# Three last-step additions on GpSimd, two last-step stores on ScalarE's queue, and one weight-scale transpose a run later

## The chip, the cores and the metric

The kernel runs on one core of a Trainium2 chip. A core has TensorE (matrix products into PSUM), VectorE and ScalarE (element-wise work, both read PSUM and SBUF), GpSimd (element-wise work on SBUF, and a DMA queue of its own) and SyncE (SP), which here only issues DMAs. Each engine works through its own instructions in program order and waits for others through semaphores. The metric is the device time of one execution in microseconds; the number for a kernel is the median of its runs. The time before is 871.42 us, median of 3 runs (871.37 to 873.0).

## The reference

`x` has 2048 rows of 640 values. After a layer norm without weights, two branches use the same normalized rows:

```python
xn = layernorm(x)
# A: attention, 32 heads of 192, keys and values are the last 512 of a cache of 2048
q = (xn @ wq) in heads;  k, v = last 512 rows of k_cache, v_cache
s = (softmax(q @ k.T * 192 ** -0.5) @ v, heads joined) @ wo
# B: gated unit, 640 -> 1536 -> 640
h = sigmoid(xn @ w_gate) * (xn @ w_up)
g = silu(h @ w_down)
out = x + s * g
```

There is no causal mask: every query sees all 512 keys. Everything is bfloat16 outside.

## The kernel before, in words

The schedule is written out by hand; each engine's order is the program's order. The work has three stages.

**Gated unit, first half** (to about 112 us). Row blocks of 512 are normalized, transposed and multiplied with `w_gate` and `w_up`; `h` is stored to DRAM.

**Attention** (to about 638 us). There are 16 runs, numbered r = 0 to 15, two (pi = 0 and 1) for each of eight groups g of four heads. A run has 16 score steps, k = 0 to 15 (`stage_s`, line 652), and eight products with V (`stage_pv`, line 669). Beside step k, `phase_s` (line 828) issues the query products of the next run and all side work. Queries are computed with seven products of sub-blocks where eight would be usual, in float16. Therefore the query weights are scaled by a power of two, one scale for two groups. Such a scale is made in two parts. `set_scale` (line 207) reduces partial sums on VectorE, broadcasts the value into `mx_b`, and has SP issue a 128 x 128 DMA transpose into `mx_row` (line 213). `set_scale2` (line 215) reduces that row on VectorE and makes the scale and its inverse. The dictionaries `sets` and `sets2` (lines 750 and 751) say at which (run, step) each part of the second to fourth scale stands. The scale of groups 4 and 5, the third, is first used in run 5, when ScalarE scales the weights of group 4 (line 240) among the products with V.

SP's queue carries the transposes of the attention output (line 690) and their stores (line 697), the loads of K (`load_k`, line 157) and V, the other transposes and weight loads; GpSimd's queue carries the loads of the query weights. In a run with pi = 0, step 2 issues the load of K for the next group, and step 12 scales it on VectorE (`scale_k`, line 167).

**Dense stage** (the rest). `steps` (line 770) lists 24 steps: 16 of kind O, the attention output times `wo`, and eight of kind D, `h` times `w_down`. Each takes two row tiles and does its product with seven products of sub-blocks (`product`, line 1003) in four PSUM results; two or three are kept on ScalarE first (`keep`, line 1013) and added by VectorE later. `result` (line 1033) finishes a block of one row tile (i = 0 or 1) and one column half (LEFT or RIGHT). In the second half of the O steps (m of 8 and more) it does, on VectorE: add the kept part (line 1060, where there is one), multiply by a scale and the gate (`gated`, line 991), add `acc` (line 1062, float32 inputs, bfloat16 output). The scratch `tmps` has four buffers in turn. Other O steps store a whole row tile from GpSimd's queue (line 1066); the last step stores each block as it is ready, from SP's queue (line 1064). The order in the last step is (0, LEFT), (1, RIGHT), (0, RIGHT), and (1, LEFT), which has nothing kept to add and is cut into two half-blocks of 160 columns (line 1156): five stores.

Of the kernel before, what the change touches and what calls it, by code (L numbers as in the profile page):

```python
# [9 lines left out]
ALU = mybir.AluOpType  # L10
# [7 lines left out]
def kernel(  # L18
# [13 lines left out]
    nc = tc.nc  # L32
    P = 128
# [3 lines left out]
    of = out.flatten_outer_dims()  # L37
# [54 lines left out]
    DN = D // 2  # L92
# [180 lines left out]
    with ExitStack() as bctx:  # L273
# [198 lines left out]
        for s in range(NST):  # L472
# [4 lines left out]
            for f in range(NF):  # L477
# [16 lines left out]
                if s + 1 < NST:  # L494
                    t = (s + 1) * TQ
# [251 lines left out]
    scans_pv.update({(4 + n, 7): 15 + n for n in range(NCD)})  # L747
    scans_load = {(0, 6): (11, 5), (1, 4): (12, 4), (2, 4): (13, 5), (3, 4): (14, 4)}
    scans_load.update({(4 + n, 4): (15 + n, 5 - n % 2) for n in range(NCD)})
    sets = {(1, 1): 1, (4, 1): 2, (9, 1): 3}  # L750
    sets2 = {(1, 12): 1, (5, 0): 2, (9, 12): 3}
    scale_s = {0: 2, 3: 3, 15: 4}
    q_after = {1: (0,), 2: (1,), 3: (2,), 4: (3,), 5: (4,), 6: (5, 6), 8: (7,), 10: (8,), 12: (9,), 14: (10,)}

# [24 lines left out]
    def tiles_of(j):  # L779
        kind, m = steps[j]  # L780
        if kind == "D":
            return (m, TQ + m) if m < TQ else (TQ + m, 2 * TQ + m)
        pi, q = divmod(m % 8, TQ)
        return [(2 * pi + i) * TQ + q for i in range(2)]
# [175 lines left out]
    acc = {t: acc_pool.tile([P, D], F32, name=f"acc{t}") for t in order}  # L960
# [29 lines left out]
    def gated(dst, src, gate):  # L990
        nc.vector.scalar_tensor_tensor(dst, src, descale, gate, op0=ALU.mult, op1=ALU.mult)  # L991
# [21 lines left out]
    def keep(b, dst):  # L1013
        nc.scalar.activation(dst, ps_all[:, b, 0:DN], AF.Copy)
# [9 lines left out]
    NP = len(steps)  # L1024
    tmp_at = [0, 0, 0]

    def turn_of(k, rows_):
        tmp_at[k] += 1
        return rows_[(tmp_at[k] - 1) % len(rows_)]
# [3 lines left out]
    def result(j, i, d, b, more, n0=0, n1=DN):  # L1033
        kind, m = steps[j]
        t = tiles_of(j)[i]
        ps, tt = ps_all[:, b, n0:n1], nc.vector.tensor_tensor
        if kind == "D":
            if t not in gate_of:
                gate_of[t] = turn_of(1, gate_rows)
            if more is not None:  # L1040
                v = turn_of(2, down_tmps)
                tt(v, ps, more[:], ALU.add)
                ps = v
            nc.scalar.activation(gate_of[t][:, d], ps, AF.Silu, scale=g_scale)
            if (i, d) in ((0, RIGHT), (1, LEFT)):
                nc.gpsimd.dma_start(gB_d[t * P:(t + 1) * P, :], gate_of[t])
            return
        d = slice(d.start + n0, d.start + n1)
        if m < 8:
            if more is None:  # L1050
                keep(b, acc[t][:, d])
            else:
                tt(acc[t][:, d], ps, more[:], ALU.add)
            return
        gate, o_sb = gx_rows[1, t]
        tmp = turn_of(0, tmps)[:, 0:n1 - n0]
        if more is None:
            gated(tmp, ps, gate[:, d])
        else:
            tt(tmp, ps, more[:], ALU.add)  # L1060
            gated(tmp, tmp, gate[:, d])
        tt(o_sb[:, d], tmp, acc[t][:, d], ALU.add)  # L1062
        if j == NP - 1:
            nc.sync.dma_start(of[t * P:(t + 1) * P, d], o_sb[:, d])
        elif (i, d) in ((0, RIGHT), (1, LEFT)):
            nc.gpsimd.dma_start(of[t * P:(t + 1) * P, :], o_sb)

# [30 lines left out]
    for j in range(NP):  # L1098
# [38 lines left out]
        side(j, 3)  # L1137
        product(j, Z, "A12", 3, True)
        result(j, 0, LEFT, Z, p1s)
        scales(4)  # L1140
        side(j, 4)
        product(j, X, "S3", 4, False)
        result(j, 1, RIGHT, X, p5s)
        scales(5)
        if more:
# [6 lines left out]
        side(j, 6)  # L1152
        product(j, Y, "S4", 5, False)
        result(j, 0, RIGHT, Y, u2s)
        side(j, 7)
        cuts = (0, DN) if more else (0, DN // 2, DN)
# [42 lines left out]
```

## Time and profile before

| quantity | value |
|---|---|
| median of 3 runs | 871.42 us (871.37 to 873.0) |
| the profiled execution's own time | 872.36 us |
| its span, first to last instruction | 870.2 us |
| granted TensorE clock, mean | 0.999 |
| TensorE busy | 863.0 us |
| VectorE busy | 674.5 us |
| ScalarE busy | 628.5 us |
| GpSimd busy | 234.3 us |
| bytes moved by DMA | 175.97 MB |

In the profile PE is TensorE, PEld its weight loads, DVE VectorE, ACT ScalarE, POOL GpSimd, SP SyncE; a q behind a name is that engine's instruction queue, SPq for example the DMAs that SP issues. L1007 is line 1007 of the kernel. An instruction's line gives its start, its duration, engine, line, operation, output<-inputs, sizes and count; in brackets stands the idle time before it and what ended it. The chain is the work that ended last, followed back step by step to what released it. Times in the stage view are microseconds from the span's start.

### The profile page before, as it was taken

How to read it: one execution, taken by the hardware profiler on the slowest of the kernel's cores; microseconds unless marked ns; L12 is line 12 of the kernel's file. 1: busy time of each engine (PE TensorE's matmuls, PEld its weight loads, DVE VectorE, ACT ScalarE, POOL GpSimd, SP SyncE). 2: the span in 40 equal slices, each digit the busy share in tenths (PEclk: the TensorE clock that was granted, in tenths of full speed). 3: DMA queues.
4: the chain of work that ended last, by engine and by line, in shares of the span. 5: the costliest groups of instructions: out<-in, count | busy, mean ns of one | idle time of the engine just before them, and what ended most of it. 6: DMA issues, size and time to landing. Idle time of an engine off the chain costs nothing.

```text
span 870.2 us, 19053 instructions
## 1 busy us (share of the span) xinstructions
PE 863.0 (99%) x7557; PEld 570.7 (66%) x7557; DVE 674.5 (78%) x1148; ACT 628.5 (72%) x783; POOL 234.3 (27%) x320
## 2 busy tenths in 40 slices
PE   9999999999999999999999999999999999999998
PEld 5444447576678676676676676676777777777775
DVE  6586767777877867867877867888788778889997
ACT  4766568899799799799789688647556566766552
POOL 0085076062362352352352452300000011000000
PEclk9999999999999999999999999999999999999999
DMA  9894993998998987998988967997795977676641
GB/s 280 188 248 113 240 244 82 236 138 236 219 158 233 256 170 194 223 172 225 206 144 214 199 106 193 237 206 248 163 277 179 300 240 224 212 269 222 226 134 35
DMA packets 258872, 175.97 MB, mean 202 GB/s; under 512 B 162976, under 2 KB 241440, under 8 KB 258784
## 3 DMA queue, kind: packets, MB, share of 16 engines
q1 hardware_dynamic: 253248, 157.26, 73.2%
q0 software_dynamic: 5536, 17.50, 10.0%
q8 instruction: 59, 0.97, 0.5%
q14 instruction: 29, 0.24, 0.1%
HBM read 101.71 MB, written 36.70 MB: 159 GB/s over the span
## 4 chain that ended last, share of the span: by engine, by line
PE 97%; DVE 1%; DMA 1%; SPq 0%; issue 0%; ACT 0%; DVEq 0%
PE ps_all L1007 26%; PE ps_all L569 21%; PE ps_all L677 20%; PE ps_all L663 19%; PE ps_all L484 11%; PE ps_all L387 1%; DMA kraw<-in_A_k_cache_dram 0%; DVE stats L349 0%; DVE arm L991 0%; DMA x_sb<-in_A_x_dram 0%; DVE arm L1062 0%; DVE arm L1060 0%; DVE qp L590 0%; DVE xn L364 0%; SPq L213 0%
## 5 line engine op out<-in xcount | busy, mean ns | idle before, releaser
L667 ACT ACTIVATE E<-ps_all 128x1024 bf16<-128x1024 f32 x256 | 251.4, 1023 | 92.4 <-PE ps_all L663 90.4
L663 PE MATMUL ps_all<-qT,kT 64*128 64x512 bf16 x1536 | 198.1, 376 | 0.0
L677 PEld LDWEIGHTS <-E 128*128 128x128 bf16 x2048 | 169.7, 98 | 9.2 <-issue 9.2
L677 PE MATMUL ps_all<-v_sb,E 128*128 128x193 bf16 x2048 | 174.3, 247 | 0.9 <-DVE qT L607 0.8
L607 DVE TENSOR_TENSOR qT<-ps_all,qp 128x512 bf16<-128x512 f32 x174 | 115.7, 688 | 48.2 <-PE ps_all L569 38.8
L1007 PEld LDWEIGHTS <-mid 128*128 128x128 f16 x1236 | 120.3, 98 | 46.0
L663 PEld LDWEIGHTS <-kT 64*128 64x128 bf16 x1536 | 86.5, 94 | 77.5 <-issue 3.5
L590 DVE COPY qp<-ps_all 128x512 f32<-128x512 f32 x150 | 100.5, 687 | 42.2 <-PE ps_all L569 42.2
L684 DVE TENSOR_TENSOR o_st<-ps_all,rden 128x768 bf16<-128x768 f32 x128 | 122.6, 958 | 4.4
L569 PE MATMUL ps_all<-mid 64*128 64x512 f16 (+1 forms) x840 | 106.3, 376 | 0.0
L569 PE MATMUL ps_all<-mid,arm 64*128 64x512 f16 (+1 forms) x840 | 105.5, 376 | 0.0
L569 PEld LDWEIGHTS <-mid 64*128 64x128 f16 x840 | 50.4, 94 | 42.0 <-issue 1.4
L569 PEld LDWEIGHTS <-arm 64*128 64x128 f16 x840 | 47.1, 94 | 44.6 <-issue 0.2
L1007 PE MATMUL ps_all<-arm,mid 128*128 128x320 f16 x480 | 70.4, 299 | 0.0
L808 ACT ACTIVATE mid<-mid,w_sc 128x1536 f16<-128x1536 bf16 (+1 forms) x43 | 61.4, 1451 | 0.0
L240 ACT ACTIVATE mid<-mid,w_sc 128x1536 f16<-128x1536 bf16 x37 | 58.1, 1571 | 1.1 <-DVE w_sc L218 0.7
L1007 PE MATMUL ps_all<-op,mid 128*128 128x320 f16 (+1 forms) x408 | 58.1, 295 | 0.0
L490 DVE TENSOR_TENSOR hT_sb<-ps_all,sig_sb 128x512 bf16<-128x512 f32 x48 | 32.8, 686 | 28.4 <-PE ps_all L484 20.8
L489 ACT ACTIVATE sig_sb<-ps_all 128x512 bf16<-128x512 f32 x48 | 28.4, 596 | 35.3 <-PE ps_all L484 33.8
L258 POOL TENSOR_TENSOR mid<-mid 128x384 f16<-128x384 f16 x20 | 18.1, 906 | 120.1 <-ACT mid L240 119.1
L1007 PE MATMUL ps_all<-mid 128*128 128x320 f16 x348 | 49.9, 299 | 0.0
L258 POOL TENSOR_TENSOR arm<-mid 128x384 f16<-128x384 f16 x20 | 18.1, 907 | 114.5 <-ACT mid L240 113.5
(183 smaller groups left out, 1093.1 us busy)
## 6 DMA issues: line engine op xcount, KB each, us to landing
oT_d<-oT SPq DMA_DIRECT2D x64, 384.0 KB, 4.9
mid<-oT_d SPq DMA_DIRECT2D x46, 384.0 KB, 4.0
mid<-in_A_wq_dram POOLq DMA_DIRECT2D x64, 192.0 KB, 6.7
arm<-in_A_wo_dram SPq DMA_DIRECT2D x16, 480.0 KB, 6.2
h_d<-hT_sb SPq DMA_DIRECT2D x16, 384.0 KB, 4.4
kraw<-in_A_k_cache_dram SPq DMA_DIRECT2D x32, 192.0 KB, 3.2
v_sb<-in_A_v_cache_dram SPq DMA_DIRECT2D x32, 192.0 KB, 5.5
arm<-in_A_wq_dram SPq DMA_DIRECT2D x15, 384.0 KB, 5.3
```

The source lines that it names most:

```text
L240: nc.scalar.activation(raw.bitcast(F16), raw, AF.Copy, scale=w_ups[g // 2])
L258: tt(TB, part_w(g, c, a, 1, 1), part_w(g, c, a, 0, 1), ALU.subtract)
L484: nc.tensor.matmul(gu[:, i, :], lhsT=w[:, c, f * P:(f + 1) * P], rhs=xnT[s][:, c, :], start=(c == 0), stop=(c == NCD - 1),)
L569: nc.tensor.matmul(ps_all[:, b, :], lhsT=w(r, c), rhs=x[r, c, :], start=(first and k == 0), stop=(k == len(cs) - 1), skip_group_check=True,)
L590: nc.vector.tensor_copy(dst, part(b))
L607: nc.vector.tensor_tensor(q_out(i, u, pp), part(b), t, ALU.add)
L663: nc.tensor.matmul(ps[:, b, :], lhsT=kT[h, c * PC + j, :], rhs=qT_t[r][i, j][h, pp, :], start=(j == 0), stop=(j == PC - 1),)
L667: nc.scalar.activation(E_t[r, i, pp][:, c, :, :], ps, AF.Exp, scale=scale_qk)
L677: nc.tensor.matmul(o_ps[:, q // 2, q % 2, 0:DH + 1], lhsT=E[:, c, h, q * P:(q + 1) * P], rhs=vt[:, c, 0:DH + 1], start=(c == 0), stop=(c = ...
L684: nc.vector.tensor_tensor(o_st[:, :, h * DH:(h + 1) * DH].rearrange("p (b i) d -> p b i d", b=2), o_ps[:, :, :, 0:DH], rden[:].to_broadcas ...
L808: eng.activation(t, t.bitcast(BF16), AF.Copy, scale=up)
L1007: nc.tensor.matmul(ps_all[:, b, d0:d1], lhsT=a[:, c, :], rhs=w[:, c, d0:d1], start=(start and c == 0), stop=(c == nk - 1), skip_group_chec ...
```

## The change

Three edits. (1) The two parts of the third scale move from run 4, step 1 and run 5, step 0 to run 5, steps 1 and 12, the same steps that the second and fourth scale have in runs 1 and 9. (2) In the last dense step the addition of `acc` goes from VectorE to GpSimd for the three blocks that have a kept part; the two half-blocks stay on VectorE. (3) Two of the last step's five stores go from SP's queue to ScalarE's: that of (0, RIGHT) and that of the first half-block.

```diff
-    sets = {(1, 1): 1, (4, 1): 2, (9, 1): 3}
-    sets2 = {(1, 12): 1, (5, 0): 2, (9, 12): 3}
+    sets = {(1, 1): 1, (5, 1): 2, (9, 1): 3}
+    sets2 = {(1, 12): 1, (5, 12): 2, (9, 12): 3}
...
-        tt(o_sb[:, d], tmp, acc[t][:, d], ALU.add)
+        if j == NP - 1 and more is not None:
+            nc.gpsimd.tensor_tensor(o_sb[:, d], tmp, acc[t][:, d], ALU.add)
+        else:
+            tt(o_sb[:, d], tmp, acc[t][:, d], ALU.add)
         if j == NP - 1:
-            nc.sync.dma_start(of[t * P:(t + 1) * P, d], o_sb[:, d])
+            eng = nc.scalar if i == 0 and d.start > 0 or n0 == 0 and n1 < DN else nc.sync
+            eng.dma_start(of[t * P:(t + 1) * P, d], o_sb[:, d])
```

## The prediction

> **What bounds the kernel now.** I read the head of the page first, then the chain, then the length of each attention run, then the two places that the diff touches.
>
> ```profile
> span 870.2 us, 19053 instructions
> PE 863.0 (99%) x7557; PEld 570.7 (66%) x7557; DVE 674.5 (78%) x1148; ACT 628.5 (72%) x783; POOL 234.3 (27%) x320
> ...
> PE 97%; DVE 1%; DMA 1%; SPq 0%; issue 0%; ACT 0%; DVEq 0%
> ```
>
> TensorE is busy for 863.0 of 870.2 us, and the change removes no matmul. So it can only move the 7.2 us in which TensorE stands. Attention run r goes from one first score product (L663) to the next; the stage view, TensorE alone, shows length, TensorE busy time (count), clock, DMA share and GB/s of runs 1, 4, 5 and 9:
>
> ```profile
> 156.50:189.17 32.67, 32.67 (x331) 1.00 0.98 208
> 254.60:288.38 33.78, 32.93 (x331) 1.00 0.93 194
> 288.38:321.10 32.72, 32.72 (x332) 1.00 0.95 209
> 419.43:452.14 32.71, 32.71 (x331) 1.00 0.96 186
> ```
>
> Run 4 is 1.06 us longer than run 5. It is the run with the third scale's transpose; runs 1 and 9 hold the second's and fourth's and lose nothing. The chain inside run 4, SP's queue, VectorE's wait, and the transfer rate from 268 to 278 us in quarter microseconds:
>
> ```profile
> 272.30 0.97 SPq L213
> ...
> 273.33 0.56 SPq L161
> ...
> 273.94 3.05 DMA kraw<-in_A_k_cache_dram
> ```
> ```profile
> 271.92 1.35 SPq L213 DMA_TRANSPOSE mx_row<-mx_b  x1
> ```
> ```profile
> 276.52 0.93 DVE L170 TENSOR_SCALAR k_sb<-kraw,w_sc 128x768 bf16<-128x768 bf16 x2 [1.19 <-DMA kraw<-in_A_k_cache_dram]
> ```
> ```profile
> GB/s 294 327 342 352 373 244 303 301 304 307 310 303 295 273 284 290 336 369 358 376 361 359 310 294 187 71 131 172 212 39 184 326 393 387 369 356 393 234 37 0
> ```
>
> The transpose holds SP for 1.35 us just ahead of the K load. VectorE then stands 1.19 us for that K, with query copies behind it that free PSUM, and TensorE loses 1.06 us. From 274.0 to 275.75 us the rate falls to a mean of 142 GB/s.
>
> The other place is the end, first VectorE, then SP:
>
> ```profile
> 865.02 0.55 DVE L991 SCALAR_TENSOR_TENSOR arm<-arm,w_sc 128x320 f32<-128x320 f32 x1
> 865.60 0.49 DVE L1062 TENSOR_TENSOR arm<-arm,acc 128x320 bf16<-128x320 f32 x1
> 866.08 0.38 DVE L991 SCALAR_TENSOR_TENSOR arm<-ps_all,w_sc,arm 128x160 f32<-128x160 f32 x1
> 866.50 0.33 DVE L1062 TENSOR_TENSOR arm<-arm,acc 128x160 bf16<-128x160 f32 x1
> 866.74 0.38 DVE L991 SCALAR_TENSOR_TENSOR arm<-ps_all,w_sc,arm 128x160 f32<-128x160 f32 x1
> 867.15 0.33 DVE L1062 TENSOR_TENSOR arm<-arm,acc 128x160 bf16<-128x160 f32 x1
> ```
> ```profile
> 866.85 0.99 SPq L1064 DMA_DIRECT2D out_dram<-arm  x2
> ```
>
> Up to 864.49 VectorE follows TensorE, one block per 1.63 us. The last two half-blocks leave TensorE at about 865.2 and 866.04 and find VectorE busy. The last store is issued at 867.51, lands 1.5 us later, and the closing barriers end at 870.2.
>
> **The transpose, run 4 to run 5.** What leaves run 4: four small VectorE operations after step 1, SP's 1.35 us, and the dip in the rate. Against the 345 GB/s on either side the dip costs 1.75 x (1 - 142/345) = 1.03 us of transfer. K's two halves landed at 276.5 and 277.0 and were wanted at 275.33 and about 275.8; 1.03 us earlier they come at 275.5 and 276.0. About 0.2 us of the wait is left (run 8, with a wait of 0.30 us, is 0.2 us long), worth some 0.1 us. Gain 0.95 us. Upper end: 1.06, the whole excess. Lower end: 0.1, if K must land behind the O stores anyway, the last of which landed at 275.9; in runs 2, 6 and 8 K's first half came 0.4 to 0.6 us behind that store. I take a value near the upper end because those runs show no such dip.
>
> What arrives in run 5: the same four operations, the transpose on SP at about 297.5, and at step 12 the three that read it. Behind it on SP stand one scan load, three output-weight loads, one down-weight load and the two K transposes. SP is idle from 300.79 to 306.04 there, 5.25 us for 1.35. VectorE reaches step 12 some 20.7 us into the run, at 309; the row lands at most 4.5 us after issue, at 302. I cost it at nothing, as runs 1 and 9 measure (32.67 and 32.71). If the cover fails, the price is run 4's 1.06.
>
> **Three additions on GpSimd.** They remove three 0.49 us operations from VectorE. The first two free only time that TensorE's pace leaves idle. The third, at 865.60, is in the final queue: the rest moves up 0.51 us. But GpSimd's add runs beside it, and these two block each other:
>
> ```profile
> 47.16 0.90 POOL L259 TENSOR_TENSOR mid<-mid 128x384 f16<-128x384 f16 x1
> ...
> 47.21 2.20 DVE L455 TENSOR_TENSOR mid<-mid,x_odd 64x2560 f16<-64x2560 bf16 x1
> ```
> ```profile
> 107.20 1.47 DVE L455 TENSOR_TENSOR mid<-mid,x_odd 64x2560 f16<-64x2560 bf16 x1
> ```
>
> The same operation takes 1.47 us alone and 2.20 when GpSimd is 0.85 us from its end: 0.73 more, the remainder less 0.12. L447 at 56.82 repeats it (0.64 left, 0.52 more). A product with PSUM as one input (L490 at 45.49, beside GpSimd's copies) keeps its 0.69.
>
> No row has a float32 add on GpSimd. The rows give 0.906 us for 384 elements; by elements, 320 take 0.755; unscaled, 0.906; by bytes, 1.51. GpSimd starts 0.06 us after its releaser (146.50 + 0.61 to 147.17). So add 3 runs from 865.63 to 866.39 or 866.54. VectorE's first half-block scales out of PSUM from 865.57 to 865.95, unhindered, and its addition at 865.99 has two SBUF inputs: 0.28 to 0.43 us of waiting. It ends at 866.60 to 866.75; the last half-block's two operations take 0.65 more as before, so VectorE ends at 867.25 to 867.40 instead of 867.48. Gain 0.08 to 0.23; I take 0.15. Adds 1 and 2, from 862.38 and 864.00, end before VectorE's next two-SBUF operations at 863.39 and 865.02. The reuse of the first scratch buffer makes the last scaling wait for add 1, over 3 us earlier.
>
> [...]
>
> **Two stores on ScalarE's queue.** ScalarE ends its work at 860.0. Its first store waits for add 3, its second is queued behind it; only the end of the program waits for both. SP's five stores took 0.33 us each without queueing, so nothing is gained. At SP's price they go at 866.5 and 866.9 and land by 868.5, before the last SP store at 867.28 to 867.43 (868.8 to 868.95). No row has a ScalarE store. Bounds: 1.5 us to land, as SP's at this very moment; 4.0, as GpSimd's output stores (L1066), taken beside much other traffic, which would put the end at 870.5 instead of 869.0. I take SP's, same data and moment. [...]
>
> **Sum.** -0.95 - 0.15 + 0.02 = -1.1 us. The profiled execution took 872.36 (870.2 plus 2.16 around it) and would take 871.3. It stands 0.94 above the median of 871.42, so the median run may hold less of the stall; I still set the whole sum against the median: 870.3.
>
> **Rivals.**
> A. K lands behind the stores anyway, or run 5 pays run 4's price: gain 0.1 plus 0.15, 871.2. For: the order on the queue. Against: runs 1 and 9.
> B. GpSimd's add does not hold up VectorE's, and the waits of runs 8 and 10 (0.2 and 0.13 over 32.71) shrink as K's schedule shifts: 0.95 + 0.51 + 0.3, 869.7. For: the collision rows are 16-bit. Against: their regularity.
> C, the other side. GpSimd's float32 add takes 1.51 us. Each add then reaches into VectorE's next scaling: 0.38 late in the second block, 0.75 in the third, 1.03 at the half-block; VectorE ends at 868.75, 1.27 later. Less 0.95 that is 0.3 slower, 871.7. It decides from about 1.4 us per add; above 2.0 the kernel is over 0.2% slower.
> D. ScalarE's store takes 4.0 us: 1.5 later at the end, less 0.95: 872.0.
>
> **How the numbers follow.** Chances: forecast 0.52, A 0.15, B 0.15, C 0.11, D 0.07. No change can be told from a change within 0.2%, 1.74 us, here: 869.68 to 873.16. Faster takes B, which lies at the bound, and the forecast's low edge, where the waits of runs 8 and 10 shrink too: 0.25. Slower takes C's far end, D with a longer landing, and an A in which runs 5 and 6 both pay: 0.11. The rest, 0.64, is within. The range takes in A, C and most of B's surroundings: 869.3 to 871.9; the forecast's own is 869.9 to 870.8.
>
> **What would show it.** Run 4 at 32.7 to 32.9 us with at most 0.3 us of waiting for K, and run 5 still at 32.7 with the transpose near 297; a GpSimd add of 0.75 to 0.9 us; VectorE's first half-block addition stretched from 0.33 to 0.6 to 0.8; the last VectorE operation 1.2 to 1.35 us after the last matmul, now 1.44; ScalarE's stores landed before SP's last. It is wrong if run 5 or 6 grows by a microsecond, if a GpSimd add takes over 1.4, or if the span ends on ScalarE's queue.

## The result, and the profile after

The changed kernel takes 875.81 us (median of 6 runs, 875.57 to 875.87); the kernel before, on the same chip, 871.48 us. The ratio is 1.0046, 95% interval 1.0033 to 1.0059. The forecast was 870.3 us, the range 869.3 to 871.9, and "slower" had a chance of 0.11. The prediction was wrong.

The head of the page after, and its chain by engine, hardly show it. TensorE is as busy as before (862.4 us beside 863.0), yet the span is 3.8 us longer:

```profile
span 874.0 us, 19042 instructions
PE 862.4 (99%) x7548; PEld 567.1 (65%) x7557; DVE 672.3 (77%) x1145; ACT 628.3 (72%) x783; POOL 236.9 (27%) x323
...
PE 98%; DMA 0%; DVE 0%; SPq 0%; issue 0%; ACT 0%
```

The stage view of TensorE, runs 4 and 5 of the kernel after (length, busy time, clock, DMA share, GB/s):

```profile
254.82:287.53 32.71, 32.71 (x331) 1.00 0.88 193
287.53:320.25 32.72, 32.72 (x332) 1.00 1.07 215
```

Run 4 has lost its 1.06 us of excess and run 5, now with the transpose, has gained none. By the last matmul the kernel after is a microsecond ahead: it ends at 865.02, against 866.04 before. The time is lost behind it. From the timeline of the end, GpSimd's third addition, VectorE's first and last operation on the half-blocks, and ScalarE's two stores:

```profile
864.61 0.86 POOL L1063 TENSOR_TENSOR arm<-arm,acc 128x320 bf16<-128x320 f32 x1 [0.77 <-DVE arm L991]
865.04 0.38 DVE L991 SCALAR_TENSOR_TENSOR arm<-ps_all,w_sc,arm 128x160 f32<-128x160 f32 x1 [0.51 <-PE ps_all L1007]
...
865.49 0.86 ACTq L1068 DMA_DIRECT2D out_dram<-arm  x2
...
866.11 0.32 DVE L1065 TENSOR_TENSOR arm<-arm,acc 128x160 bf16<-128x160 f32 x1
```

All work is done at 866.43, and the last store, issued at 866.5, has landed at 868.0. The span ends at 874.0. What lies between are instructions that are not counted as busy: each engine runs a `DRAIN`, then the engines meet at semaphores (in both kernels 12 semaphore events of SP, 4 of GpSimd and 2 of each other engine). The source view of the closing lines gives, for the drains of GpSimd and SP, the shortest, median and longest duration in ns and the first and last start in us. SP's first drain starts when its last store has landed, 1.5 us after its issue (867.5 to 869.0 before, 866.5 to 868.0 after). Before:

```profile
L1194 POOLq DRAIN  x3: 40/160/8316, 858.6 to 870.0; - x3
L1194 SPq DRAIN  x3: 7/7/7, 869.1 to 869.7; - x3
```

And after:

```profile
L1198 POOLq DRAIN  x3: 40/93/8664, 864.6 to 873.7; - x3
L1198 SPq DRAIN  x3: 7/7/7, 868.0 to 873.5; - x3
```

GpSimd's first drain is the long one. Before, it ended at 858.6 + 8.3 = 866.9, behind a last store that SP saw land at 869.0: hidden, with 2.1 us of cover. After, it starts with the third addition and ends at 873.2, and the span ends 0.8 us later. In both kernels it ends 7.8 us after GpSimd's last instruction: a store of 0.54 us from 858.58 before, an addition ending at 865.47 after.

### The profile page after: what moved, and what is told of

Read it like the earlier page. It is cut to its first block, busy times and chain, and to the rows that moved or that the text cites. A ratio compares the mean times of both kernels' runs of the same rounds, so it can differ in the third digit from the quotient of the medians.

```text
span 874.0 us, 19042 instructions
## 1 busy us (share of the span) xinstructions
PE 862.4 (99%) x7548; PEld 567.1 (65%) x7557; DVE 672.3 (77%) x1145; ACT 628.3 (72%) x783; POOL 236.9 (27%) x323
## 3 DMA queue, kind: packets, MB, share of 16 engines
q0 software_dynamic: 5536, 17.50, 10.1%
## 4 chain that ended last, share of the span: by engine, by line
PE 98%; DMA 0%; DVE 0%; SPq 0%; issue 0%; ACT 0%
PE ps_all L1007 26%; PE ps_all L569 21%; PE ps_all L677 20%; PE ps_all L663 19%; PE ps_all L484 11%; PE ps_all L387 1%; DMA x_sb<-in_A_x_dram 0%; SPq L322 0%; DVE stats L349 0%; SPq L301 0%; DVE arm L991 0%; DVE arm L1065 0%; ACT mid L402 0%; PE ps_all L400 0%; DVE xn L364 0%
## 5 line engine op out<-in xcount | busy, mean ns | idle before, releaser
L569 PEld LDWEIGHTS <-mid 64*128 64x128 f16 x840 | 48.1, 94 | 44.3 <-issue 1.0
```

The source lines that it names most:

```text
L569: nc.tensor.matmul(ps_all[:, b, :], lhsT=w(r, c), rhs=x[r, c, :], start=(first and k == 0), stop=(k == len(cs) - 1), skip_group_check=True,)
```

## The experiments

Theory G: GpSimd's closing drain reaches 7.8 us past its last instruction, and the additions moved that instruction to the end. Rival S: the closing wait comes with the DMAs on ScalarE's queue. A third idea is that the wait grows with the work given to GpSimd.

**The three edits apart.** Each kernel has one edit of the change, or all but one.

```diff
 e1_transpose_only: edit 1 alone
+    sets = {(1, 1): 1, (5, 1): 2, (9, 1): 3}
+    sets2 = {(1, 12): 1, (5, 12): 2, (9, 12): 3}
 e2_adds_only: edit 2 alone
+            nc.gpsimd.tensor_tensor(o_sb[:, d], tmp, acc[t][:, d], ALU.add)
 e3_stores_only: edit 3 alone
+            eng = nc.scalar if i == 0 and d.start > 0 or n0 == 0 and n1 < DN else nc.sync
 e4_no_adds: edits 1 and 3
```

> Only the third scale's two parts are moved to run 5, steps 1 and 12; the end is as before. Theory G (GpSimd's closing drain reaches 7.8 us past its last instruction, and the three additions moved that instruction to the end) and rival S (the closing wait comes with a DMA on ScalarE's queue) both expect 1.06 us less than before, 870.4 us, with run 4 at 32.71 us instead of 33.78. If instead the moved transpose cost something later, it would be 871.4 or more.

> Only the three additions go to GpSimd; all five stores stay on SP's queue, the transpose stays in run 4. G: GpSimd's last instruction ends some 0.5 us before TensorE's last matmul plus 1 us, its drain 7.8 us later, and the end comes about 4.9 us later than before: 876.4 us. S: no ScalarE store, so no closing wait: 871.5 us.

> Only two stores go to ScalarE's queue. G: GpSimd's last instruction is its old store at about 859, its drain ends at 867 unseen, 871.5 us, no change. S: 4.9 us more, 876.4 us.

> The change without the three additions (transpose and stores moved). G: the transpose's 1.06 us are gained whole, 870.4 us. S: as the whole change, 875.8 us.

| kernel | median, us | ratio to before | 95% interval |
|---|---|---|---|
| before | 871.28 | | |
| transpose only | 871.39 | 1.0001 | 0.9992 to 1.0010 |
| additions only | 876.27 | 1.0052 | 1.0035 to 1.0069 |
| stores only | 871.35 | 1.0000 | 0.9990 to 1.0009 |
| transpose and stores | 871.33 | 0.9999 | 0.9990 to 1.0008 |

The additions alone bring the whole loss; ScalarE's stores bring none, so S falls. But both theories also missed: of the 1.06 us by which run 4 was long in the profiled execution, moving the transpose brings nothing in the medians. The profile of the kernel with only the stores moved shows why. Its transpose is still in run 4; its stage and SP's transpose there:

```profile
254.93:287.72 32.79, 32.79 (x331) 1.00 0.94 194
```
```profile
268.98 1.56 SPq L213 DMA_TRANSPOSE mx_row<-mx_b  x1
```

Run 4 is 0.08 us long, not 1.06. In the profiled execution of before, SP reached this transpose at 271.92, 2.9 us later, since the work ahead of it on the queue took longer: the second transpose of the attention output 6.30 us instead of 4.80, the four loads of V 4.18 instead of 3.04. The kernel with only the additions, profiled, has 32.79 in run 4 too. So the stall of 1.06 us was that of one execution (872.36 us, against medians of 871.2 to 871.5 in all comparisons), not of the usual one. Nor does a stall there need this transpose: in the profiles of the two kernels under "Two tries" below, which have it in run 5, run 4 is 0.36 and 0.27 us long, VectorE waiting 0.56 and 0.46 us for loads on SP's queue.

**When GpSimd ends, and how much it does.** All three are the whole change with another condition on the addition; the third gives GpSimd only a copy of one column.

```diff
 e5_first_add
-        if j == NP - 1 and more is not None:
+        if j == NP - 1 and more is not None and i == 0 and d.start == 0:
 e6_two_adds
-        if j == NP - 1 and more is not None:
+        if j == NP - 1 and more is not None and (i == 1 or d.start == 0):
 e7_tiny_op: the additions on VectorE, and
+        if j == NP - 1 and i == 0 and d.start > 0:
+            nc.gpsimd.tensor_copy(tiny[:], tmp[:, 0:1])
```

> The whole change, but only the first of the three additions is on GpSimd. G (a fixed 7.8 us after GpSimd's last instruction, whatever it was): that instruction ends 2.75 us before TensorE's last matmul, the drain ends 5.05 us behind it and the time is 872.7 us, 3.1 less than the whole change. If the closing wait came with any use of GpSimd in the last step, and not with when it ends, it would be 875.8 us as for the whole change.

> The whole change with the first two additions on GpSimd, the third on VectorE. G: the last GpSimd instruction ends 1.2 us before TensorE's last matmul; 874.3 us. If the wait grows with the work given to GpSimd (one third for each addition): 874.4 us, not to be told from G here; the next run tells them apart.

> All additions are back on VectorE; GpSimd only copies one column (128 x 1) of the third block's scaled result to a scratch tile that nobody reads. G: its last instruction then ends about 0.2 us before TensorE's last matmul, and the time is about 875.2 us with nearly no GpSimd work in the step. If the wait grows with the work: about 871.5 us.

Measured: 872.98, 874.26 and 875.63 us, beside 871.19 for the kernel before; ratios 1.0025 (1.0014 to 1.0037), 1.0033 (1.0017 to 1.0049) and 1.0051 (1.0028 to 1.0073). G had 872.7, 874.3 and 875.2; the third is 0.4 above, and its copy ends 0.1 us behind the last matmul instead of 0.2 ahead. A copy of one value per partition costs as much as three additions (ratio 1.0051 beside 1.0046), and it ends nearly as late (864.92 us beside 865.47). GpSimd's timeline and its drains in that kernel:

```profile
864.48 0.44 POOL L1064 COPY tiny<-arm 128x1 f32<-128x1 f32 x1 [6.58 <-DVE arm L992]
```
```profile
L1198 POOLq DRAIN  x3: 40/102/7931, 864.8 to 873.2; - x3
```

It ends at 864.92, the drain at 872.7: 7.8 us again. So the moment at which GpSimd ends sets the loss, not the work it was given. In the profiles of all seven kernels whose drain ends behind the last store, the span ends 0.77 to 0.79 us after the drain.

**What the drain is for.** In the next two kernels GpSimd issues fewer DMAs; the additions stay as in the change.

```diff
 e8_no_pool_dma: no DMA of the program from GpSimd
-        load_raw(1 + (c + 3) // NCD, (c + 3) % NCD, nc.gpsimd)
+        load_raw(1 + (c + 3) // NCD, (c + 3) % NCD, nc.sync)
-            load_raw(n // NCD, n % NCD, nc.gpsimd)
+            load_raw(n // NCD, n % NCD, nc.sync)
 e8_no_pool_dma and e12_no_late_pool_dma
-                nc.gpsimd.dma_start(gB_d[t * P:(t + 1) * P, :], gate_of[t])
+                nc.sync.dma_start(gB_d[t * P:(t + 1) * P, :], gate_of[t])
-            nc.gpsimd.dma_start(of[t * P:(t + 1) * P, :], o_sb)
+            nc.sync.dma_start(of[t * P:(t + 1) * P, :], o_sb)
```

> The whole change, but every DMA that GpSimd issued (query weights, gate rows, output rows) goes to SP's queue; the three additions stay on GpSimd. Only the closing drain is read here; the attention stage may be slower for SP's longer queue. If the drain flushes what GpSimd's DMAs left, it shrinks to under 1 us behind the last addition. If it belongs to GpSimd's own instructions, it stays at 7.8 us.

> The whole change, but the DMAs that GpSimd issues in the dense stage (gate rows and output rows) go to SP's queue; its 64 loads of query weights stay, the last of them some 310 us before the end. If the 7.8 us drain is owed by any DMA that GpSimd issued in the program, it stays: 875.8 us. If it is owed only by recent ones, it shrinks to about 1 us behind the last addition, and the time is about 871.3 us, as without the additions.

GpSimd's drains, first with no DMA from GpSimd in the program:

```profile
L1198 POOLq DRAIN  x3: 34/78/959, 872.6 to 876.7; - x3
```

And with the 64 weight loads only:

```profile
L1198 POOLq DRAIN  x3: 40/102/6220, 866.9 to 873.6; - x3
```

The last additions end at 873.45 and 867.76; with the starts read from the trace to the nanosecond, the drains reach 0.07 and 5.33 us past them. The second was neither of its two expected values. Set beside the number of DMAs that GpSimd issued in the whole program, the three kernels stand on a line: none, 0.07 us; 64, 5.33 us; 94 (64 + 16 + 14), 7.77 us; that is 0.08 us for each. Of what 94 DMAs add, 64 would keep 5.31 us in proportion to their number, 5.61 by bytes (12.58 of 17.50 MB) and 5.77 by packets on GpSimd's queue (4096 of 5536). The reach repeats within 0.02 us in the twelve profiles with 94 DMAs, so the count fits and bytes or packets alone do not. But no run changed the count alone: the 64 are loads of 192 KB, the other 30 rows of 160 KB, and a price that differs by kind is not ruled out.

The times of these two kernels (878.71 in one run; 877.88, from 875.64 to 880.96) are no verdict on the drain: SP's longer queue delays other work. In the first, attention's run 0 takes 38.0 us instead of 32.9, with an 8.06 us load of query weights in the chain; in the second, the chain holds an 8.19 us load of gate rows in the dense stage.

**The half-blocks.** Why did VectorE not end sooner behind TensorE? This kernel is the whole change with the first half's result written between the two halves' matmuls.

```diff
-        product(j, X, "A22", 6, False, cuts)
         for n0, n1 in zip(cuts, cuts[1:]):
+            product(j, X, "A22", 6, False, (n0, n1), n1 == DN)
             result(j, 1, LEFT, X, None, n0, n1)
```

> The whole change, but in the last step the first half-block's result is written into the program between the matmuls of the two half-blocks. If VectorE's first half-block scaling waits for the last matmul of both halves because both were issued ahead of it, it now starts some 0.45 us before TensorE ends instead of 0.02 us after; its addition then meets GpSimd's third addition and is stretched from 0.33 us to about 0.7. If the wait has another reason, the scaling starts behind TensorE's end as before. The time stays near 875.8 us, since the drain sets the end.

It takes 875.92 us in one run. Its end, in the timeline:

```profile
864.57 0.38 DVE L991 SCALAR_TENSOR_TENSOR arm<-ps_all,w_sc,arm 128x160 f32<-128x160 f32 x1
864.74 0.86 POOL L1064 TENSOR_TENSOR arm<-arm,acc 128x320 bf16<-128x320 f32 x1 [0.77 <-DVE arm L991]
864.99 0.79 DVE L1066 TENSOR_TENSOR arm<-arm,acc 128x160 bf16<-128x160 f32 x1
865.00 0.99 PE L1007 MATMUL ps_all<-op,mid 128*128 128x160 f16 x12 [0.70 <-DVE arm L991]
```

The scaling now starts as soon as VectorE is free, at 864.57. So in the change, where VectorE stood 0.51 us and the scaling started at 865.04, 0.02 us behind the last matmul, it waited for the matmuls of both halves. The addition behind it meets GpSimd's and is stretched from 0.33 to 0.79 us: of the 0.61 us that GpSimd's had left, it was held 0.46. And TensorE's second half now waits 0.70 us for that scaling, so nothing is won: the written order trades one wait for the other.

**Two tries at a better end.** Both have the moved transpose, and GpSimd and SP as before. One leaves the last block whole; the other adds the third block's kept part to `acc` ahead of time and writes the half-block's result between the halves.

```diff
 e9_uncut
-        product(j, X, "A22", 6, False, cuts)
-        for n0, n1 in zip(cuts, cuts[1:]):
-            result(j, 1, LEFT, X, None, n0, n1)
+        product(j, X, "A22", 6, False)
+        result(j, 1, LEFT, X, None)
 e11_pre_add: ahead of the last step's first block
+            gated(ahead_t, u2s[:], gx_rows[1, t][0][:, RIGHT])
+            nc.vector.tensor_tensor(acc[t][:, RIGHT], ahead_t, acc[t][:, RIGHT], ALU.add)
...
-        result(j, 0, RIGHT, Y, u2s)
+        result(j, 0, RIGHT, Y, u2s if more else None)
```

> The moved transpose alone, all work on VectorE and SP as before, and the last block not cut in half: one scaling of 0.54 us and one addition of 0.49 behind TensorE's end instead of two and two (1.42), and a store that lands 0.1 us later. If VectorE's queue at the end sets the time: 0.2 to 0.3 us less than the kernel before, 871.1 us.

> The moved transpose; the third block's kept part is scaled and added to acc in VectorE's idle 2 us ahead of the last step's first block, so that one operation of 0.49 us less stands behind its matmul; the first half-block's result stands between the two halves' matmuls. GpSimd and ScalarE's queue are used as before. VectorE should end some 0.95 us behind TensorE instead of 1.43, and the time be 0.5 us less than before, 870.8 us. If the closing sequence and not VectorE sets the end: no change.

The uncut kernel takes 871.00 us beside 871.54, ratio 0.9993 (0.9984 to 1.0002). That is 0.54 us less, about twice what was expected, and not told from no change; the medians of the spans, 869.2 and 869.5, differ by 0.3. The other takes 871.47 (871.0 to 874.48), ratio 1.0003 (0.9994 to 1.0012). In its profile VectorE ends only 0.79 us behind TensorE, better than the 0.95 expected, but TensorE's second half waits 0.63 us for the first half's scaling, about as much as was won.

## Why the prediction was wrong

**The additions on GpSimd: the step that failed.** The prediction let the path to the end run from VectorE's last operation over the last store to the closing barriers. It counted the additions' own 0.86 us (0.755 to 0.906 was forecast), the 0.06 us to their start, and their collision with VectorE, and closed with a gain of 0.15 us. It did not count that the span ends only when GpSimd has drained: that term stood at nothing, without a reason. The drain was in the trace of before, from 858.6 to 866.9, with 2.1 us of cover. That cover let GpSimd work until some 4.8 us before the last matmul (866.9 - 859.12 = 7.8 back from 869.0 is 861.2, against 866.04). The additions moved its last instruction to 0.45 us behind that matmul. Rival C bounded the price of an addition, not the moment at which it ends. This edit alone brings the whole loss (5.0 us), and the change without it is within 0.1% of the kernel before.

**The gain of 0.15 us in that step** was also wrong, by its ready times: the first half-block was taken to be free at 865.2, in the clock of before, when its own matmuls end. It is free only when both halves are done, at 866.04; before, it was scaled at 866.08, so VectorE's third addition was in the way by at most 0.04 us. VectorE ends 1.41 us behind TensorE after, 1.44 before: 0.03 us gained, not 0.15. The collision seen in the 16-bit rows (the remainder less 0.12 us) was there in float32 too (0.33 to 0.79 with the scaling set early, the remainder of 0.61 less 0.15), but in the change itself the half-block's addition comes as GpSimd's ends (865.46 beside 865.47) and is not stretched: 0.33 us. The measured 0.86 us for one addition lies between 0.755, scaled by elements, and the unscaled 0.906.

**The transpose.** That run 5 would cover it was right: in the profile after, run 5 stays at 32.72 us with the transpose at 298.79, and run 4 is 32.71. The term was mis-sized: 0.95 us from one execution that stood 0.94 above the median. The prediction noted that difference, then set the whole sum against the median. In two other profiles with the transpose in run 4 the excess is 0.08 us, and the medians show 0.0. Nor is it shown that the transpose made all of the 1.06 us: in the uncut kernel SP's queue was about as slow ahead of the load of K (6.53 us for the second transpose of the attention output, 4.05 for the four loads of V), and run 4 lost 0.36 us there without this transpose. By this comparison of two executions the transpose is worth an estimated 0.7 us in such a one (1.06 - 0.36). Rival A gave the stall a chance to stay or to move; that it might not be there was left out.

**The stores** were right: 1.6 to 1.7 us to land, landed about 867.5, half a microsecond ahead of SP's last; alone, ratio 1.0000. No run shows the sum's 0.02 us, put there for one more queue to wait for at the end: SP's closing lines hold 12 semaphore events of 17 to 28 ns with ScalarE's stores as without them, and in the time, with an interval of 0.9990 to 1.0009, it could not be seen.

**What of the 4.3 us.** In the profile after, without the drain the end would come an estimated 1.2 us behind the last store's landing, as before (870.2 - 869.0): 868.0 + 1.2 = 869.2. The drain puts it at 874.0, 4.8 us later. In medians the additions alone cost 5.0 us and the whole change 4.3. Of this difference of 0.7, 0.2 lies between the two medians of the kernel before (871.28 and 871.48). Another 0.36 lies outside the spans: an execution takes 2.10 to 2.14 us more than its span with the additions alone, and 1.72 to 1.78 with the whole change. The medians of the spans themselves, 874.15 and 874.05, differ by 0.1. Why the part outside the span differs between the kernels stays open.

## What to carry to other kernels

Before work is moved to another engine near the end, read the closing lines of the trace: when that engine's last instruction ends now, how long its drain reaches past it, and how much of that the last store hides (here 859.12 us, 7.8 us, and all of it with 2.1 us of cover). A stall read from one profile is a stall of that execution; where its own time stands above the median by about as much as the stall, do not count on it in the median, which here held none of it. The two halves of one product in one PSUM result became ready together when both were issued before the first was read (VectorE started on the first 0.02 us behind the last matmul of both); when the first was read in between, the second's matmuls waited for that read, 0.70 and 0.63 us in the two kernels that did so.

## What the runs showed that I had not expected

GpSimd's closing drain reaches past its last instruction by an amount that follows what GpSimd did in the whole program, not what it did last. It was 7.75 to 7.77 us in all twelve profiles with 94 DMAs from GpSimd, whether the last instruction was a store, an addition or a copy of one column; 5.33 us with 64 DMAs, the last of them issued at 519.4, some 350 us before the end; 0.07 us with none. The number of DMAs fits these to 0.02 us, their bytes or packets alone miss by 0.3 to 0.4; what GpSimd does in that time no run shows.
